# Scores and values times W1 in eight array tiles of 64 rows by 32 columns, and the token work over two tiles at once

## The chip, the cores and the metric

The kernel runs on one core of a Trainium2 chip. The metric is the device time in microseconds (us). Before the change three runs gave 532.68 us (median; 532.6 to 533.12). TensorE is PE in the profile (PEld is its loading of weights), VectorE is DVE, ScalarE is ACT, GpSimd is POOL, SyncE is SP; SP issues nearly all loads, POOL the stores of the output.

## The reference, cut to what matters

Attention over 32 memory slots per head, then a mixture of experts with one expert per token:

```
a   = softmax of phi over the 576 positions           # 8 batches, 8 heads, 576 x 32
k_m = a.T @ k ; v_m = a.T @ v                         # 32 x 64 per head
s   = softmax over the 32 slots of (q @ k_m.T / 8)    # 576 x 32 per head
x   = s @ v_m, the heads side by side                 # 4608 tokens x 512
logits = cosine of x with 8 expert vectors / tau ; e = argmax ; gate = softmax at e
out = gate * (relu(x @ w1[e]) @ w2[e])                # w1 512 x 1024, w2 1024 x 512
```

## The kernel before

One batch of 576 tokens goes through three stages.

`memories(b)` (lines 203 to 274) turns the exponentials of phi (`te`), multiplies them with k and v in column tiles of 32 (`slots`, line 219, tile `acc`), scales (`block`, lines 229 and 230) and turns the result per head pair (`flip`), so that `kT` and `vT` hold for each head pair c a 128-row block: rows 0 to 63 the first head's 64 features, rows 64 to 127 the second's, with columns for 32 slots of each and zeros in the two off-diagonal quarters.

`tokens(b)` (lines 276 to 401) works on five tiles of 128 tokens (`T0`; the fifth overlaps the fourth by half). `scores(i)` multiplies q (as weights, 128 x 128) with `kT` (64 columns) for four head pairs, line 291; DVE takes the maximum and subtracts it, ACT the exponential (lines 295 to 298). `weights(i)` divides by the sum (303 to 306). `turn(i)` transposes the weights on PE (312); ACT copies them to `ah` and DVE takes the rest `al` (315, 316), two parts so that a product in the faster 32-bit form keeps its accuracy. `attend(i)` (325) multiplies them with `vh`, `vl`, and DVE forms the logits and norms (328 to 331). Then follow the choice of the expert (`key`, 352 to 365) and the gates (374 to 400).

The expert's stage is where the values enter: `first` (432 to 466) computes G = `vT` times W1 (line 441, tile `pg`, four PSUM tiles of 512 columns, two column tiles of 64 each), splits it into `gh` (ACT, 444) and `gl` (DVE, 445), and multiplies G with the weights of the tokens (line 454, tile `ph`, 16 groups of six matmuls). ACT and DVE form relu and its rest (457, 458). `second` (468 to 482) multiplies with W2 (line 476, tile `py`, five tiles of 8 x 3 matmuls), ACT scales by the gate (480), POOL stores (488). W2 is split by `split_w` within `first`.

Order: everything is written out by hand. The loop of lines 613 to 631 runs `first(b)` and `second(b)` and, after each group of matmuls in `first` and each second one in `second` (each one in batch 0), takes one step of the generator `ahead(b)`, which runs `memories(b+2)` and `tokens(b+2)`; a step is what lies between two `yield`s. The four `pg` groups of batches 1 and later have no such steps between them. All engines work through their instructions in the order written. Every matmul on plain 32-bit numbers counts as two instructions of PE.

PSUM holds two buffers for the attention (`pt`), three for `pg`, `ph` and `py` (`mm`), two banks `po` for `attend` and one for `acc`.

Of the kernel before, what the change touches and what calls it, by code (L numbers as in the profile page):

```python
# [30 lines left out]
def sqrt(nc, pool, out, ss, shape, tag):  # L31
# [6 lines left out]
    for k in range(3):  # L38
        nc.vector.reciprocal(out=r, in_=a)
        nc.vector.scalar_tensor_tensor(out=r, in0=r, scalar=0.5, in1=ss, op0=ALU.mult, op1=ALU.mult)  # L40
        nc.vector.scalar_tensor_tensor(out=out if k == 2 else a, in0=a, scalar=0.5, in1=r, op0=ALU.mult, op1=ALU.add)


class Kernel:
# [4 lines left out]
    def __init__(self, ctx, tc, phiT, qT, kv, kvt, emb, tau, w1, w2, out):  # L49
# [20 lines left out]
        self.kT = st([P, NC, D], F32, name="kT")  # L70

# [45 lines left out]
    def load_router(self):  # L117
        nc, st = self.nc, self.st.tile
        self.em = st([E, DM], F32, name="em")
        nc.scalar.dma_start(self.em, self.emb)  # L120
        self.tv = st([E, 1], F32, name="tv")
        nc.scalar.dma_start(self.tv, self.tau.broadcast_to((E, 1)))

    def router(self):
# [4 lines left out]
        sq = st([E, DM], F32, name="sq")  # L129
# [34 lines left out]
    def load_q(self, b):  # L164
        if b < B:
            self.nc.sync.dma_start(self.q(b), self.qT[b])
# [36 lines left out]
    def memories(self, b, pt):  # L203
# [11 lines left out]
        def slots(g, *ks):  # L215
            for k in ks:
# [40 lines left out]
        slots(1, 2, 3, 4)  # L257
        block(1)
        self.load_kv(b + 1)
        yield  # L260
# [15 lines left out]
    def tokens(self, b):  # L276
# [3 lines left out]
        qt = self.q(b)  # L280
        a = {}
        lg = wk([P, NT, E], F32, tag="lg", name=f"lg{b}")
        ss = wk([P, NT], F32, tag="ss", name=f"ss{b}")

# [15 lines left out]
        def weights(i):  # L300
            x = a[i]
            z = wk([P, H], F32, tag="z", name=f"z{b}_{i}")
# [5 lines left out]
        def turn(i):  # L308
            t = self.pt([P, NG, P], f"ta{b}_{i}")
            x = a[i]  # L310
            for g in range(NG):
                nc.tensor.transpose(t[:, g], x[:, 4 * g : 4 * g + 4].rearrange("p h m -> p (h m)"), self.ident)
            o = P if i < 4 else 64
            to = slice(T0[i] + P - o, T0[i] + P)
            nc.scalar.copy(ah[:, :, to], t[:, :, P - o :])
            nc.vector.tensor_tensor(out=al[:, :, to], in0=t[:, :, P - o :], in1=ah[:, :, to].bitcast(F32), op=ALU.subtract)

        def attend(i):

            po = self.po[:, i % 2, : NC * (D + E)]  # L320
            to = slice(T0[i], T0[i] + P)
            for g in range(NG):
                w = slice(2 * g * (D + E), 2 * (g + 1) * (D + E))
                for k, (x, v) in enumerate(((ah, self.vh), (al, self.vh), (ah, self.vl))):
                    nc.tensor.matmul(po[:, w], lhsT=x[:, g, to], rhs=v[:, w], start=k == 0, stop=k == 2)  # L325
            po = po.rearrange("p (c m) -> p c m", c=NC)
            x = a.pop(i).rearrange("p (c j) m -> p c (j m)", c=NC)
            nc.vector.tensor_reduce(out=lg[:, i], in_=po[:, :, D:].rearrange("p c e -> p e c"), axis=AX.X, op=ALU.add)
            nc.vector.tensor_reduce(out=m[:, i : i + 1], in_=lg[:, i], axis=AX.X, op=ALU.max)
            nc.vector.tensor_scalar(out=oh[:, i], in0=lg[:, i], scalar1=m[:, i : i + 1], scalar2=None, op0=ALU.is_equal)  # L330
            nc.vector.tensor_tensor_reduce(  # L331
                out=x, in0=po[:, :, :D], in1=x, scale=1.0, scalar=0.0, op0=ALU.mult, op1=ALU.add, accum_out=ss[:, i : i + 1]
            )

        m = wk([P, NT], F32, tag="m", name=f"m{b}")
        oh = wk([P, NT, E], BF16, tag="oh", name=f"oh{b}")

        key = self.po[:, 1, 504:]
        for k in range(NT + 4):
            if k < NT:  # L340
                scores(k)
            if 0 <= k - 1 < NT:
                weights(k - 1)
            if k < NT + 3:
                yield
            if 0 <= k - 2 < NT:
                turn(k - 2)
            if 0 <= k - 3 < NT:
                attend(k - 3)
            if k == NT + 3:  # L350
                for i in range(-1, NT):
# [312 lines left out]
```

## Time and profile before

| | us |
|---|---|
| median of three runs | 532.68 |
| the profiled execution | 532.79 |
| its span | 530.8 |
| busy PE, DVE, ACT within the span | 495.4, 309.7, 199.8 |

The span is from the first to the last instruction of the program that the profile shows; 1.99 us of the profiled execution lie around it. The busy time of PE counts a matmul from its start to its modelled end, so that consecutive matmuls overlap: what a matmul costs is read from the distance between the starts.

### The profile page before, as it was taken

The numbers are of one execution on the slowest core, as the hardware profiler recorded it, in microseconds if no ns is written. First come the engines' busy times: TensorE is split into PE (matmuls) and PEld (weight loads), VectorE is DVE, ScalarE is ACT, GpSimd is POOL, SyncE is SP. The second block draws the span as 40 slices with busy tenths as digits, with TensorE's granted clock in tenths as the row PEclk, the third lists the DMA queues.
The fourth block names the chain that finished last, engine by engine and source line by source line (L and its number), as shares of the span: only waits on it lengthen the run. The fifth ranks groups of instructions, "written<-read, shape, count | busy, mean of one in ns | idle before, by whom it ended". The sixth has DMA issues, their size and how long they took to land.

```text
span 530.8 us, 9294 instructions
## 1 busy us (share of the span) xinstructions
PE 495.4 (93%) x3396; PEld 406.1 (76%) x3396; DVE 309.7 (58%) x1016; ACT 199.8 (38%) x509; POOL 23.7 (4%) x48
## 2 busy tenths in 40 slices
PE   4685987998999999999999999999999999999994
PEld 3574676786788877988788877988788878887883
DVE  4677868187368636775468636776468548206500
ACT  4332435222563226522563226522563127216411
POOL 1000000000000010000000010000000010010000
PEclk9877877999999999999999999999999999999998
DMA  8976345960595319571595319571525117610011
GB/s 270 343 259 225 107 153 198 328 223 38 187 297 186 132 41 329 182 248 41 178 307 186 130 41 326 184 249 41 184 88 176 42 40 249 199 59 12 10 51 32
DMA packets 36817, 87.18 MB, mean 164 GB/s; under 512 B 7832, under 2 KB 7832, under 8 KB 35744
## 3 DMA queue, kind: packets, MB, share of 16 engines
q1 hardware_dynamic: 33792, 77.08, 43.6%
q0 software_dynamic: 2944, 9.44, 5.0%
q8 instruction: 29, 0.48, 0.4%
q14 instruction: 20, 0.16, 0.1%
q10 hardware_dynamic: 32, 0.02, 0.0%
HBM read 66.60 MB, written 19.92 MB: 163 GB/s over the span
## 4 chain that ended last, share of the span: by engine, by line
issue 62%; PE 20%; DVE 10%; POOL 3%; ACT 2%; DMA 1%; SPq 0%; POOLq 0%; ACTq 0%; DVEq 0%
PE py L476 7%; PE ph L454 4%; POOL out_dram L488 3%; PE sc L291 2%; PE acc L219 2%; PE po L325 2%; PE pg L441 1%; DMA kl<-kvt 1%; DVE ea L306 1%; PE te L212 1%; DVE ea L297 1%; DVE z L303 1%; DVE ea L331 1%; DVE hl L458 1%; DVE mx L295 1%
## 5 line engine op out<-in xcount | busy, mean ns | idle before, releaser
L476 PE MATMUL py<-wh,hh 128*128 128x512 f32 x320 | 130.7, 408 | 0.0
L476 PE MATMUL py<-wh,hl 128*128 128x512 f32 x320 | 125.3, 392 | 0.0
L476 PE MATMUL py<-wl,hh 128*128 128x512 f32 x320 | 125.2, 391 | 0.0
L454 PE MATMUL ph<-aT,gh 128*128 128x288 f32 x512 | 113.8, 314 | 4.1 <-DVE hl L458 4.1
L454 PEld LDWEIGHTS ph<-aT,gh 128*128 128x128 f32 x512 | 82.5, 193 | 15.2 <-DVE gl L445 5.7
L458 DVE SCALAR_TENSOR_TENSOR hl<-ph,hh 128x288 fp32r<-128x288 f32 x128 | 57.6, 454 | 34.1 <-ACT hh L457 31.4
L454 PE MATMUL ph<-aT,gl 128*128 128x288 f32 x256 | 76.6, 299 | 0.0
L480 ACT ACTIVATE ys<-py,gate 128x512 f32<-128x512 f32 x40 | 27.4, 685 | 126.1 <-PE py L476 70.1
L476 PEld LDWEIGHTS py<-wh,hl 128*128 128x128 f32 x320 | 60.4, 189 | 13.3
L476 PEld LDWEIGHTS py<-wh,hh 128*128 128x128 f32 x320 | 60.5, 189 | 10.9 <-issue 1.0
L476 PEld LDWEIGHTS py<-wl,hh 128*128 128x128 f32 x320 | 60.6, 190 | 9.8
L457 ACT ACTIVATE hh<-ph 128x288 fp32r<-128x288 f32 x128 | 52.1, 412 | 28.1 <-PE ph L454 28.0
L445 DVE TENSOR_TENSOR gl<-pg,gh 128x512 fp32r<-128x512 f32 x32 | 22.1, 691 | 65.9 <-ACT gh L444 65.9
L454 PEld LDWEIGHTS ph<-aT,gl 128*128 128x128 f32 x256 | 49.3, 193 | 0.0
L430 DVE TENSOR_TENSOR wl<-w2s,wh 128x512 fp32r<-128x512 f32 x64 | 44.2, 690 | 2.5
L488 POOL DMA_DIRECT2D out_dram<-ys x40 | 22.0, 550 | 500.8 <-ACT ys L480 428.8
L298 ACT ACTIVATE ea<-ea 128x256 f32<-128x256 f32 x40 | 16.7, 417 | 62.8 <-DVE ea L297 62.8
L291 PEld LDWEIGHTS sc<-kT,qt 128*128 128x128 f32 x280 | 36.2, 196 | 4.2 <-issue 1.8
L429 ACT CAST wh<-w2s 128x512 fp32r<-128x512 f32 x64 | 39.3, 614 | 0.0
L291 PE MATMUL sc<-kT,qt 128*128 128x64 f32 x280 | 36.5, 275 | 0.8 <-DVE vl L273 0.4
L325 PE MATMUL po<-vh,aT 128*128 128x144 f32 x160 | 31.6, 292 | 4.5 <-DVE ss L331 4.0
L441 PE MATMUL pg<-w1s,vT 128*64 128x512 f32 x128 | 31.7, 630 | 0.0
(112 smaller groups left out, 520.1 us busy)
## 6 DMA issues: line engine op xcount, KB each, us to landing
kx<-kv SPq DMA_DIRECT2D x64, 256.0 KB, 5.3
w1s<-w SPq DMA_DIRECT2D x32, 512.0 KB, 5.7
w2s<-w SPq DMA_DIRECT2D x32, 512.0 KB, 4.9
ad<-aT SPq DMA_DIRECT2D x16, 576.0 KB, 6.7
out_dram<-ys POOLq DMA_DIRECT2D x32, 256.0 KB, 2.3
qt<-qT SPq DMA_DIRECT2D x7, 1152.0 KB, 5.6
ex<-phiT SPq DMA_DIRECT2D x16, 288.0 KB, 3.6
kl<-kvt SPq DMA_DIRECT2D x16, 128.0 KB, 5.0
```

Of the source, the lines that this page charges most:

```text
L291: nc.tensor.matmul(sc[:, 2 * c : 2 * c + 2], lhsT=qt[:, c, T0[i] : T0[i] + P], rhs=self.kT[:, c], start=True, stop=True)
L325: nc.tensor.matmul(po[:, w], lhsT=x[:, g, to], rhs=v[:, w], start=k == 0, stop=k == 2)
L429: self.nc.scalar.copy(self.wh[:, j], self.w2s[:, j])
L430: self.nc.vector.tensor_tensor(out=self.wl[:, j], in0=self.w2s[:, j], in1=self.wh[:, j].bitcast(F32), op=ALU.subtract)
L441: nc.tensor.matmul(p[64 * k : 64 * k + 64], lhsT=vT[:, 2 * g + k, :D], rhs=self.w1s[:, 2 * g + k, f], start=True, stop=True)
L445: nc.vector.tensor_tensor(out=gl[:, g, f], in0=p, in1=gh[:, g, f].bitcast(F32), op=ALU.subtract)
L454: nc.tensor.matmul(p, lhsT=w[:, g, fs], rhs=x[:, g, to], start=g == 0 and k == 0, stop=g == 1 and k == 2)
L457: nc.scalar.activation(self.hh[:, f, to], p, AF.Relu)
L458: nc.vector.scalar_tensor_tensor(out=self.hl[:, f, to], in0=p, scalar=0.0, in1=self.hh[:, f, to].bitcast(F32), op0=ALU.max, op1=ALU.subtract)
L476: nc.tensor.matmul(p, lhsT=h[:, f, to], rhs=w[:, f], start=f == 0 and k == 0, stop=f == 7 and k == 2)
L480: nc.scalar.activation(y, p, AF.Copy, scale=gate[:, i : i + 1])
L488: self.nc.gpsimd.dma_start(self.out[r + o : r + P], y[o:])
```

## The change

Scores: q becomes the moving operand. For each head one matmul with 64 rows (its features) and 32 columns (its slots) runs over 512 tokens, then a second piece over the last 64; the result, slots by tokens, is copied by ACT to `sT` and transposed on PE into tokens by slots (`weigh`). The eight heads lie on eight different tiles of the array. To that end heads 4 to 7 have their two halves of the 128 rows exchanged: in `block` for k and v, and in the loads of q, W1 and the expert vectors, which become three DMAs for two (or for one).

Values times W1: the same eight tiles, in a function `project` of its own; it runs for batch b+1 within `second(b)` (after steps 19 and 27 of 40, in place of a step of `ahead` there in batch 0), for batch 0 ahead of the loop. W1 is loaded at the start of `first(b)`; W2 of batch 0 is loaded and `keep(0)` done right after the scores of batch 1.

Token work: tiles 0 and 1, 2 and 3, and 4 alone go through `weigh`, `divide`, `turn` and `attend` together; one DVE or ACT instruction covers both tiles of a pair (except the last of `attend`, one per tile), and `po` is used in both banks by a pair. `tokens` has 18 steps in place of 22, `memories` 13 in place of 12; in `memories` the products of a head group stand in one step.

```diff
+PAIRS = ((0, 1), (2, 3), (4,))
...
+def halves():
+
+    lo, hi = slice(0, 64), slice(64, 128)
+    return (slice(0, P), slice(0, P), slice(0, 2)), (lo, hi, slice(2, 4)), (hi, lo, slice(2, 4))
...
     def load_q(self, b):
         if b < B:
-            self.nc.sync.dma_start(self.q(b), self.qT[b])
+            for dst, src, c in halves():
+                self.nc.sync.dma_start(self.q(b)[dst, c], self.qT[b, src, c])
...
     def load_w1(self, e):
-        nc = self.nc
         for h in range(2):
-            for g in range(NG):
-                c, f = slice(2 * g, 2 * g + 2), slice(h * 512, h * 512 + 512)
-                nc.sync.dma_start(self.w1s[:, c, f], self.w1[bass.ds(e, 1), :, c, f].rearrange("a p c f -> (a p) c f"))
+            f = slice(h * 512, h * 512 + 512)
+            for dst, src, c in halves():
+                self.nc.sync.dma_start(
+                    self.w1s[dst, c, f], self.w1[bass.ds(e, 1), src, c, f].rearrange("a p c f -> (a p) c f")
+                )
...
-            nc.vector.tensor_scalar(out=kb[:, g], in0=self.acc[:, :, :D], scalar1=r, scalar2=None, op0=ALU.mult)
-            nc.scalar.activation(vb[:, g], self.acc[:, :, D:], AF.Copy, scale=r)
+            k, v = (x[:, g].rearrange("p (k i) d -> p k i d", i=2)[:, :, :: 1 - 2 * g] for x in (kb, vb))
+            a = self.acc.rearrange("p (k i) d -> p k i d", i=2)
+            nc.vector.tensor_scalar(out=k, in0=a[..., :D], scalar1=r, scalar2=None, op0=ALU.mult)
+            nc.scalar.activation(v, a[..., D:], AF.Copy, scale=r)
...
-        slots(0, 0, 1)
-        yield
-        slots(0, 2, 3, 4)
+        slots(0)
         block(0)
         yield
-        slots(1, 0, 1)
+        yield
         yield
         flip(0)
         yield
-        slots(1, 2, 3, 4)
+        slots(1)
         block(1)
         self.load_kv(b + 1)
+        yield
         yield
         yield
         flip(1)
...
-        def scores(i):
-            sc = self.pt([P, H, M], f"sc{b}_{i}")
-            for c in range(NC):
+        def scores(t0, t1):
+
+            ts = [self.pt([P, t1 - t0], f"ts{b}_{t0}{g}") for g in range(NG)]
+            for h in range(H):
+                g, j = divmod(h, 4)
+                c, i = divmod(h, 2)
+                r = slice(64 * (i ^ g), 64 * (i ^ g) + 64)
                 nc.tensor.matmul(
-                    sc[:, 2 * c : 2 * c + 2], lhsT=qt[:, c, T0[i] : T0[i] + P], rhs=self.kT[:, c], start=True, stop=True
+                    ts[g][32 * j : 32 * j + 32],
+                    lhsT=self.kT[r, c, 32 * i : 32 * i + 32],
+                    rhs=qt[r, c, t0:t1],
+                    start=True,
+                    stop=True,
                 )
-            mx = wk([P, H], F32, tag="mx", name=f"mx{b}_{i}")
+            for g in range(NG):
+                nc.scalar.copy(sT[:, g, t0:t1], ts[g])
+
+        def weigh(p):
+            ti = PAIRS[p]
+            n = len(ti)
+            sc = self.pt([P, n, H, M], f"sc{b}_{p}")
+            for k, i in enumerate(ti):
+                for g in range(NG):
+                    nc.tensor.transpose(
+                        sc[:, k, 4 * g : 4 * g + 4].rearrange("p h m -> p (h m)"), sT[:, g, T0[i] : T0[i] + P], self.ident
+                    )
+            sc = sc.rearrange("p k h m -> p (k h) m")
+            mx = wk([P, 2 * H], F32, tag="mx", name=f"mx{b}_{p}")[:, : n * H]
             nc.vector.tensor_reduce(out=mx, in_=sc, axis=AX.X, op=ALU.max)
-            a[i] = x = wk([P, H, M], F32, tag="ea", name=f"ea{b}_{i}", bufs=5)
+            a[p] = x = wk([P, 2 * H, M], F32, tag="ea", name=f"ea{b}_{p}", bufs=3)[:, : n * H]
...
+        def attend(p):
+
+            ti = PAIRS[p]
+            n, i = len(ti), slice(ti[0], ti[-1] + 1)
+            po = self.po[:, :n, : NC * (D + E)]
+            for k in range(n):
+                to = slice(T0[ti[k]], T0[ti[k]] + P)
+                for g in range(NG):
+                    w = slice(2 * g * (D + E), 2 * (g + 1) * (D + E))
+                    for l, (x, v) in enumerate(((ah, self.vh), (al, self.vh), (ah, self.vl))):
+                        nc.tensor.matmul(po[:, k, w], lhsT=x[:, g, to], rhs=v[:, w], start=l == 0, stop=l == 2)
+            po = po.rearrange("p t (c m) -> p t c m", c=NC)
+            x = a.pop(p).rearrange("p (t c j) m -> p t c (j m)", t=n, c=NC)
+            nc.vector.tensor_reduce(
+                out=lg[:, i], in_=po[..., D:].rearrange("p t c e -> p t e c"), axis=AX.X, op=ALU.add
...
+        scores(0, 512)
+        yield
+        scores(512, S)
+        if b == 0:
+            self.load_q(2)
+        elif b >= 2:
+            self.load_q(b + 1)
+        yield
+        for k in range(len(PAIRS) + 3):
+            if k < len(PAIRS):
+                weigh(k)
+            if 0 <= k - 1 < len(PAIRS):
+                divide(k - 1)
+            if k < len(PAIRS) + 2:
                 yield
+            if 0 <= k - 2 < len(PAIRS):
                 turn(k - 2)
+            if 0 <= k - 3 < len(PAIRS):
                 attend(k - 3)
+            if k == len(PAIRS) and b >= 1:
                 self.softmax(b + 1)
             yield
...
-    def first(self, n, at, vT):
+    def project(self, n, vT):
+
+        nc = self.nc
+        for k in range(2):
+            f = slice(512 * k, 512 * k + 512)
+            ps = [self.mm([P, 512], f"pg{n}_{k}{g}") for g in range(NG)]
+            for h in range(H):
+                g, j = divmod(h, 4)
+                c, i = divmod(h, 2)
+                r = slice(64 * (i ^ g), 64 * (i ^ g) + 64)
+                nc.tensor.matmul(
+                    ps[g][32 * j : 32 * j + 32],
+                    lhsT=vT[r, c, 32 * i : 32 * i + 32],
+                    rhs=self.w1s[r, c, f],
+                    start=True,
+                    stop=True,
+                )
+            for g in range(NG):
+                nc.scalar.copy(self.gh[:, g, f], ps[g])
+                nc.vector.tensor_tensor(
+                    out=self.gl[:, g, f], in0=ps[g], in1=self.gh[:, g, f].bitcast(F32), op=ALU.subtract
+                )
+            yield
+
+    def first(self, n, at):
 
         nc = self.nc
...
-        if n >= 5:
+        if n == 0 or n >= 4:
             steps(mem)
     for _ in mem:
         pass
     tok = k.tokens(1)
-    steps(tok, 5)
+    steps(tok, 2)
+    k.load_w2(k.expert(0))
+    k.keep(0)
+    steps(tok, 3)
+    for _ in k.project(0, k.vT[0]):
+        steps(tok)
     left = None
     for b in range(B):
         att = k.ahead(b, tok)
         tok = None
-        for n, _ in enumerate(k.first(b, k.aT[b % 2], k.vT[b % 2])):
-            if n == NG * 2 - 1 and 1 <= b < B - 1:
-                k.load_w1(k.expert(b + 1))
-            if n >= NG * 2 or b == 0:
-                steps(att)
-            if b == 0 and n == NG * 2:
-                k.load_w2(k.expert(0))
-                k.keep(0)
+        if 1 <= b < B - 1:
+            k.load_w1(k.expert(b + 1))
+        for _ in k.first(b, k.aT[b % 2]):
+            steps(att)
         if b + 1 < B:
             k.load_w2(k.expert(b + 1))
             k.keep(b + 1)
+        pro = k.project(b + 1, k.vT[(b + 1) % 2]) if b + 1 < B else iter(())
         for n, _ in enumerate(k.second(b, k.gate[:, b], k.rows(b))):
-            if b == 0 or n % 2 == 0:
+            if n in (19, 27):
+                steps(pro)
+            elif b == 0 or n % 2 == 0:
                 steps(att)
         for _ in att:
             pass
```

The functions `divide` and `turn` are the former `weights` and `turn` over a pair; `softmax(b+1)` stays behind the first `attend`. `em` and the square of the expert vectors now lie in `sT`.

## Rows read from the trace of the kernel before

**Rows 1.** The profile's page: busy time by engine, and granted clock in 40 slices.
```profile
PE 495.4 (93%) x3396; PEld 406.1 (76%) x3396; DVE 309.7 (58%) x1016; ACT 199.8 (38%) x509; POOL 23.7 (4%) x48
...
PEclk9877877999999999999999999999999999999998
```

**Rows 2.** Batches 1 and 6: length; busy PE, PEld, DVE, ACT, POOL; clock; DMA, GB/s.
```profile
137.32:197.05 59.73, 59.61 (x425) 49.22 (x424) 38.31 (x124) 24.53 (x63) 2.73 (x5) 1.00 0.54 183
...
436.02:479.75 43.73, 43.73 (x234) 36.23 (x233) 14.98 (x28) 15.73 (x33) 2.73 (x5) 1.00 0.46 154
```

**Rows 3.** Timeline of PE into batch 4: start, us, instruction, count.
```profile
316.03 0.39 PE L476 MATMUL py<-wl,hh 128*128 128x512 f32 x1
316.26 0.39 PE L476 MATMUL py<-wh,hl 128*128 128x512 f32 x1
316.58 3.65 PE L441 MATMUL pg<-w1s,vT 128*64 128x512 f32 x16
320.16 0.53 PE L454 MATMUL ph<-aT,gh 128*128 128x288 f32 x2
```

**Rows 4.** Timeline of PE, windows 316.70 to 317.00 and 324.66 to 324.70.
```profile
316.58 0.65 PE L441 MATMUL pg<-w1s,vT 128*64 128x512 f32 x2
...
324.61 0.32 PE L219 MATMUL acc<-kx,eT 128*32 128x128 f32 x4
```

**Rows 5.** Timeline of PE in batch 4: products of `memories`, transposes, scores.
```profile
321.06 0.60 PE L212 MATMUL te<-ident,ex 128*128 128x128 f32 x4
321.41 0.51 PE L454 MATMUL ph<-aT,gh 128*128 128x288 f32 x2
...
324.61 0.64 PE L219 MATMUL acc<-kx,eT 128*32 128x128 f32 x16
325.19 0.53 PE L454 MATMUL ph<-aT,gh 128*128 128x288 f32 x2
...
341.58 0.39 PE L476 MATMUL py<-wh,hl 128*128 128x512 f32 x1
341.81 1.00 PE L291 MATMUL sc<-kT,qt 128*128 128x64 f32 x8
342.62 0.48 PE L476 MATMUL py<-wh,hh 128*128 128x512 f32 x1
342.93 0.39 PE L476 MATMUL py<-wl,hh 128*128 128x512 f32 x1
```

**Rows 6.** Groups by line and shape: count, busy us, mean ns, then idle before.
```profile
L480 ACT ACTIVATE ys<-py,gate 128x512 f32<-128x512 f32 x40 | 27.4, 685 | 126.1 <-PE py L476 70.1 <-issue 51.3 <-PEq L506 4.8
...
L445 DVE TENSOR_TENSOR gl<-pg,gh 128x512 fp32r<-128x512 f32 x32 | 22.1, 691 | 65.9 <-ACT gh L444 65.9
...
L295 DVE TENSOR_REDUCE mx<-sc 128x8 f32<-128x256 f32 x40 | 16.7, 417 | 7.9 <-PE sc L291 7.7
...
L213 ACT COPY eT<-te 128x512 f32<-128x512 f32 x16 | 9.4, 588 | 1.5 <-PE te L212 1.4
```

**Rows 7.** Waits of PE in window 16 to 137: us, times, longest.
```profile
PE sc L291 <- DVE ea L297: 5.7, 2, 5.4
PE ph L454 <- DVE hl L458: 4.1, 3, 2.2
PE po L325 <- DVE ss L331: 4.0, 5, 1.5
```

**Rows 8.** Timeline of PE in batch 0.
```profile
51.65 1.98 PE L441 MATMUL pg<-w1s,vT 128*64 128x512 f32 x4
53.55 0.69 PE L312 MATMUL ta<-ident,ea 128*128 128x128 f32 x2
...
61.19 0.51 PE L454 MATMUL ph<-aT,gh 128*128 128x288 f32 x2
...
90.45 0.78 PE L476 MATMUL py<-wh,hh 128*128 128x512 f32 x1
```

More of the change, by code (lines that the diff above doesn't have):

```diff
@@ L118, in load_router @@
         nc, st = self.nc, self.st.tile
-        self.em = st([E, DM], F32, name="em")
-        nc.scalar.dma_start(self.em, self.emb)
+        self.em = self.sT[:E, 0, :DM]
+        src, dst = (x.rearrange("e (c i d) -> e c i d", c=NC, i=2) for x in (self.emb, self.em))
+        nc.scalar.dma_start(dst[:, :2], src[:, :2])
+        for i in range(2):
+            nc.scalar.dma_start(dst[:, 2:, i], src[:, 2:, 1 - i])
         self.tv = st([E, 1], F32, name="tv")
@@ L213, in turn, with slots @@
             nc.scalar.copy(eT[:, i0:i1], t[:, : i1 - i0])
-        def slots(g, *ks):
-            for k in ks:
+        def slots(g):
+            for k in range(5):
                 src = self.kx[k] if k < 4 else self.kl
@@ L279, in tokens @@
         ah, al = self.aT[b % 2]
-        qt = self.q(b)
+        qt, sT = self.q(b), self.sT
         a = {}
@@ L306, in weights @@
             nc.vector.tensor_tensor(out=x, in0=x, in1=b3(z, M), op=ALU.mult)
[L308 to L332, printed above, removed]
-            )
@@ L335, in tokens, with turn @@
[L335 to L344, printed above, removed]
+        def turn(p):
+            ti = PAIRS[p]
+            t = self.pt([P, NG, len(ti) * P], f"ta{b}_{p}")
+            for k in range(len(ti)):
+                for g in range(NG):
+                    x = a[p][:, H * k + 4 * g : H * k + 4 * g + 4].rearrange("p h m -> p (h m)")
+                    nc.tensor.transpose(t[:, g, k * P : k * P + P], x, self.ident)
+            o = 0 if p < 2 else 64
+            to = slice(T0[ti[0]] + o, T0[ti[-1]] + P)
+            nc.scalar.copy(ah[:, :, to], t[:, :, o:])
+            nc.vector.tensor_tensor(out=al[:, :, to], in0=t[:, :, o:], in1=ah[:, :, to].bitcast(F32), op=ALU.subtract)
@@ new lines, in attend @@
+        def attend(p):
+            ti = PAIRS[p]
+            n, i = len(ti), slice(ti[0], ti[-1] + 1)
[10 more added lines that the diff above has]
+                out=lg[:, i], in_=po[..., D:].rearrange("p t c e -> p t e c"), axis=AX.X, op=ALU.add
+            )
+            nc.vector.tensor_reduce(out=m[:, i], in_=lg[:, i], axis=AX.X, op=ALU.max)
+            nc.vector.tensor_tensor(out=oh[:, i], in0=lg[:, i], in1=b3(m[:, i]), op=ALU.is_equal)
+            for k in range(n):
+                nc.vector.tensor_tensor_reduce(
+                    out=x[:, k],
+                    in0=po[:, k, :, :D],
+                    in1=x[:, k],
+                    scale=1.0,
+                    scalar=0.0,
+                    op0=ALU.mult,
+                    op1=ALU.add,
+                    accum_out=ss[:, ti[k] : ti[k] + 1],
+                )
@@ L349, in tokens @@
                 attend(k - 3)
-            if k == NT + 3:
-                for i in range(-1, NT):
-                    nc.tensor.matmul(
-                        key, lhsT=self.ones, rhs=self.eb if i < 0 else oh[:, i], start=i < 0, stop=i == NT - 1
-                    )
-            if k == NT - 1:
-                if b == 0:
-                    self.load_q(2)
-                elif b >= 2:
-                    self.load_q(b + 1)
-            if k == NT and b >= 1:
+            if k == len(PAIRS) and b >= 1:
@@ L361, in tokens @@
                 self.softmax(b + 1)
             yield
+        for i in range(-1, NT):
+            nc.tensor.matmul(key, lhsT=self.ones, rhs=self.eb if i < 0 else oh[:, i], start=i < 0, stop=i == NT - 1)
         ki = wk([1, 1], I32, tag="ki", name=f"ki{b}")
@@ L430, in split_w @@
         self.nc.vector.tensor_tensor(out=self.wl[:, j], in0=self.w2s[:, j], in1=self.wh[:, j].bitcast(F32), op=ALU.subtract)
[L432 removed]
+    def project(self, n, vT):
[14 more added lines that the diff above has]
+                )
+            for g in range(NG):
+                nc.scalar.copy(self.gh[:, g, f], ps[g])
+                nc.vector.tensor_tensor(
+                    out=self.gl[:, g, f], in0=ps[g], in1=self.gh[:, g, f].bitcast(F32), op=ALU.subtract
+                )
+            yield
+    def first(self, n, at):
         nc = self.nc
         gh, gl, (ah, al) = self.gh, self.gl, at
[L436 to L446 removed]
         for s in range(2):
@@ L575, in rest @@
                 nc.vector.scalar_tensor_tensor(out=ix, in0=tok, scalar=bc, in1=ex, op0=ALU.add, op1=ALU.add)
-                for _ in self.first("r", at, vT):
+                for _ in self.project("r", vT):
+                    pass
+                for _ in self.first("r", at):
                     pass
```

25 lines of the change are left out of this document (8 added, 17 removed).

## Prediction

> **What bounds the kernel now.** I read the page first, then windows cut where a batch's first `pg` starts, then the timeline of PE in one batch, its waits, and the groups by shape for durations. The page shows PE busy for 93% of the span and at nine tenths of the full clock (2.4 GHz) or more from the eighth slice on, 93 us; ahead of that the granted clock is lower, down to 0.7 in a slice [rows 1]. The windows say that batches 1 to 5 take 59.7 us each at a granted clock of 1.00 (five rows from 59.71 to 59.77; one stands) with PE busy in all but 0.1 us of it, while DVE is busy for 38 us and ACT for 25; batch 6, which has no attention beside it, takes 43.7 us, all PE [rows 2]. So from 137 us on only fewer or shorter PE instructions make it faster, and anything that makes PE wait makes it slower by as much. The stretch before, up to 137 us, is a mixture: the PE waits of any length lie there, for DVE in nearly all cases [rows 7].
>
> **W1 in `project`.** The 16 `pg` instructions start at 316.58; with the last `py` at 316.26 and 0.23 us between `py` starts (316.03, 316.26), the engine is free at 316.49, and the next stage starts at 320.16: 3.67 us a batch [rows 3]. In the window 316.70 to 317.00 exactly two instructions are under way [rows 4], the two column tiles of 64; 16 instructions in 3.58 us are so 8 rounds of 0.45 us. After the change there are 16 instructions per half of the 1024 columns, on eight tiles: if all eight run beside each other, two rounds, 0.9 us, and I add 0.25 for entering and leaving (0.09 before the first `pg`, and 0.08 that the first matmul behind another kind costs: 342.62 to 342.93 is 0.31 against 0.23 [rows 5]) and for eight starts. Two halves: 2.3 us, a gain of 1.4 us for each of 8 batches. That four tiles run beside each other is seen: four `acc` instructions are under way together [rows 4]. That two tiles in different row halves do is seen nowhere before; the bounds are two rounds (0.9 us) and four (1.8 us), and I take two, since the tiles that the trace shows never delay each other. The drain by ACT and DVE (0.59 and 0.69 us each for 512 columns [rows 6]) moves from the start of `first` into `second`, where both have room.
>
> **Scores.** Now a tile costs 342.62 less 341.81 (0.81), plus 0.08: 0.89 us, five times 4.45 us a batch [rows 5]. After: one piece of 512 tokens as above, 1.15 us; one of 64 tokens, 16 instructions again: at least two rounds of an eighth (0.11 us), at most 0.75 us, what the 16 `acc` instructions of 128 columns take with their edges (325.19 less 324.61, and 0.17) [rows 5]; I take 0.45, the middle. And ten transposes: four `te` take 321.41 less 321.06, 0.35 us, with the edge 0.43 [rows 5]; two fours and a two are 1.1 us. Sum 2.7 us, a gain of 1.75 us a batch.
>
> **Fewer changes of kind.** `slots` of a head group stands in one step instead of two, and `turn` and `attend` in 4 places instead of 6. Each place saved is 0.17 us of edges; 0.5 us a batch with the shorter `attend` sequences counted as nothing.
>
> **Token work on DVE and ACT.** An instruction of 256 elements takes 0.42 us (`mx`), one of 512 takes 0.69 [rows 6]: two become one for 0.15 us less, seven times for two pairs, so about 2 us less of DVE a batch; ACT gets four copies (two of 0.59 and two short ones, some 1.6 us) and joins two pairs of instructions twice. In batches 1 to 5 that gains nothing by itself, since neither bounds.
>
> **New waits.** (a) The second piece of the scores needs the two PSUM buffers that the first piece filled, so PE waits for two copies of 0.59 us on ACT [rows 6] and 0.2 until the first can begin, with one `ph` group of 0.9 us in between (six matmuls, 320.16 to 321.06 [rows 3, 5]): 0.5 us. (b) A pair takes both banks of `po`. `attend(2)` can start only when DVE has read the pair before, and DVE stands behind `softmax(b+1)`, which waits for ACT. I take 0.9 us, near the mean of the five waits of `po` for `ss` in the stretch before 137 us (4.0 over 5 [rows 7]). Behind the waiting matmul stand the `py` matmuls, so PE stands still. Together 1.4 us a batch. Bounds: nothing, for PE has no such wait in batches 1 to 5 today [rows 2]; and 1.5 us at each of five places, as the longest wait of `po` for `ss` in batch 0 [rows 7], 7.5 us. I take the low one, because in batches 1 to 5 the steps lie two `py` triples (1.4 us) apart, and in batch 0 one.
>
> So a batch of 1 to 5 gains 1.4 + 1.75 + 0.5 - 1.4 = 2.2 us, five times 11 us; batch 6 gains 1.4.
>
> **Up to 137 us.** In batch 0 W1 ran at half clock: four instructions from 51.65 to 53.55, and four such parts with token work between them, until the first `ph` at 61.19 [rows 8]. After: two parts of 2.1 us at that clock in place of four of 1.9, and shorter DVE work on the tiles around them; that is 7.6 against 4.2, a gain of 3.4. The token work that stands with them has some ten DVE instructions fewer, 1.5 us. So I put the first `ph` 5 us earlier, at 56. From there to the first `py` at 90.45 [rows 8] PE waits for DVE [rows 7], which has the same splits, gates and relu rests to do: nothing. `second(0)` then holds W1 of batch 1 in its shorter form (1.4) and shorter scores, but with a step after each `py` triple the pairs wait longer: a gain of 2 with W1. Together 7 us, between none (if the chain of DVE sets the time as before) and 12 (if all of batch 0's token work shrinks as its instruction count). W1, q and the expert vectors take 3 DMAs for 2 or 1; W1 is issued a whole `first` ahead of its use, so that costs nothing in batches 1 to 5; for batch 0 it is two issues more on SP, under 1 us, inside these bounds.
>
> **Sum.** 11 + 1.4 + 7 = 19.4 us off the profiled execution, 532.79 us (0.11 over the median of the three runs): 513.4, say 513 us.
>
> **Rivals.**
> *Row halves one after the other.* Heads 0 to 3 write one PSUM bank from both row halves. If tiles of different halves wait for each other there, each piece takes four rounds: 0.9 us more, twice per batch for W1 and once, with 0.1 for the short piece, for the scores: 2.8 a batch, 14 us over five, 1.8 in batch 6, 4 before: 533 us, no change. For it: no row here shows two row halves at once. Against: the four column tiles show no coupling. The Trainium skill, TensorEngine Tiling (Array Packing), section Restrictions and Gotchas, says under PSUM pressure that different row tiles write different banks and can't access the same bank at the same time; by that rule this rival would be the outcome, and no row here tests it, as all tiles before have 128 rows.
>
> *The ring of three PSUM buffers.* `project` takes two of the three buffers while `py` fills the third. If buffers are handed out strictly in turn, the next `py` gets the one just filled and waits for ACT's `ys`, 0.69 us [rows 6], and some 0.2 of latency: 0.9 us twice in seven batches, 12.6 us: 526 us. For it: there are only three. Against: at that moment two are free or soon will be, if the next free one is taken.
>
> *Nothing waits.* The two waits cost nothing (7 us) and the start gains 12 in place of 7: 501 us. For it: PE has hardly a wait after 137 us now.
>
> *Slower: the pair chain stands in PE's order.* Weigh, divide, turn and attend of a pair are each twice as long on DVE and ACT, and PE meets them in the same order with the same few triples between. If each of five places waits 1.5 us, as `po` did once in batch 0 [rows 7], that is 7.5 in place of the 1.4 counted, 30 us over five batches: 544 us. It turns the sign from 3.9 us a batch beyond those counted (19.4 over five). Against: DVE has 21 us free in a batch.
>
> **How the numbers follow.** Forecast 0.50 (505 to 521 of its own), nothing waits 0.16, ring 0.12, row halves 0.13, pair chain 0.09. About 0.2% is what a measurement can tell from no change. Faster: 0.50 + 0.16 + 0.12 and 0.04 of the row halves, 0.82; same another 0.04 of them; slower 0.09 and their other 0.05, 0.14. The range, 500 to 532, holds the forecast, nothing waits and the ring, and reaches to the row halves.
>
> **What would show it.** `project` in two bursts of 1.1 to 1.2 us each, with eight matmuls under way at once (four: row halves in turn); `first` starting with `ph` right behind `py`; windows of batches 1 to 5 of 57.5 us; PE waits at the second piece of the scores (for ACT `sT`) and at `po` (for `ss`) of under 1 us each; no wait of `py` for `ys`; the first `ph` at about 56 us. It would be wrong if a burst takes 2 us, if PE waits add to over 4 us a batch, or if the granted clock falls below full after 100 us.

## The result and the profile after

The changed kernel takes 512.27 us (median; 511.03 to 514.8), the kernel before, measured beside it, 532.9: ratio 0.9613, 95% interval 0.9568 to 0.9658. The forecast was 513.0. The spans differ by 19.4 us (530.8 to 511.4), which is the forecast sum to the tenth; what follows shows that several of its terms were not. One of the six executions of `pg_wide` below took 933.54 us, for no reason that the record shows, and its ratio is taken without it.

The page after: TensorE is busy for 24 us less in sum; its granted clock is 8 or more tenths but for one slice, and from the eleventh slice (128 us) on 9 tenths or more up to the last slice (before: from the eighth, 93 us [rows 1]).

```profile
PE 471.0 (92%) x3540; PEld 378.3 (74%) x3540; DVE 285.9 (56%) x856; ACT 204.1 (40%) x509; POOL 23.7 (5%) x48
PEclk9988887998999999999999999999999999999998
```

Windows cut at a batch's first `ph`, for batches 1, 4, 6 and 7 (columns as in rows 2):

```profile
136.61:193.68 57.07, 56.70 (x444) 45.80 (x443) 35.38 (x104) 25.15 (x63) 2.73 (x5) 1.00 0.59 191
307.76:364.78 57.02, 56.65 (x443) 45.79 (x442) 35.38 (x104) 25.23 (x63) 2.73 (x5) 1.00 0.60 191
421.54:464.00 42.46, 42.46 (x249) 35.45 (x248) 14.80 (x28) 15.53 (x33) 2.73 (x5) 1.00 0.34 110
464.00:511.40 47.40, 40.10 (x217) 35.07 (x215) 12.22 (x24) 14.07 (x30) 3.29 (x6) 0.96 0.09 29
```

Against 59.73 and 43.73 [rows 2], batches 1 to 4 gain 2.7 us each and batch 5 3.0 (five together 13.8, from the first `ph` of batch 1 to that of batch 6); batch 6 gains 1.3. DVE has 2.9 us less to do in a batch. The remaining 4.3 us lie ahead of batch 1's first `ph` (140.91 to 136.61).

The timeline of PE around a burst of `project`, and the windows inside it with the count of `pg` under way:

```profile
291.12 0.40 PE L539 MATMUL py<-wh,hl 128*128 128x512 f32 x1
291.44 1.09 PE L492 MATMUL pg<-w1s,vT 64*32 64x512 f32 x16
292.46 0.50 PE L539 MATMUL py<-wh,hh 128*128 128x512 f32 x1
```

```profile
291.75:291.85 0.10, 0.10 (x8) 0.00 (x0) 0.00 (x0) 0.00 (x0) 1.00 0.00 0
291.95:292.00 0.05, 0.05 (x16) 0.00 (x0) 0.00 (x0) 0.00 (x0) 1.00 0.00 0
```

Eight instructions run at once, and the next eight begin before they end. The sixteen take 1.02 us up to the next `py`, which is two rounds. No `py` waits for a buffer.

The scores in batch 4, PE with the readers of `kk`, which stood one step ahead in the same pair of PSUM buffers (duration behind the start; idle time in brackets):

```profile
324.40 1.94 PE L313 MATMUL ts<-qt,kT 64*32 64x512 f32 x16
324.56 0.27 ACT L286 CAST vh<-kk 64x144 fp32r<-64x144 f32 x1 [0.75 <-DVE vl L287]
324.86 0.31 DVE L287 TENSOR_TENSOR vl<-kk,vh 64x144 fp32r<-64x144 f32 x1 [0.34 <-ACT vh L286]
325.25 0.18 PEld L313 LDWEIGHTS ts<-qt,kT 64*32 64x32 f32 x8 [0.69 <-issue]
326.27 0.54 PE L517 MATMUL ph<-aT,gh 128*128 128x288 f32 x2
327.27 0.34 PE L313 MATMUL ts<-qt,kT 64*32 64x64 f32 x16
327.54 0.53 PE L517 MATMUL ph<-aT,gh 128*128 128x288 f32 x2
```

The first piece takes 1.87 us up to the next `ph`, where the same sixteen instructions of `project` take 1.02. Its first eight instructions are heads 0 to 3, from both row halves, into the first of the two buffers; the second eight are heads 4 to 7, into the other, which `kk` held (the expectations below call these the second row half). The second eight weight loads start at 325.25, 0.08 us after the last `vl` is done (324.86 + 0.31). The list of waits does not have this one, since the first eight matmuls are still counted as busy. All that it has from 137 us on is:

```profile
PE po L369 <- DVE ss L378: 1.5, 4, 0.4
```

And in the window 16 to 137 us, beside [rows 7]:

```profile
PE po L369 <- DVE ss L378: 5.9, 5, 2.5
PE ts L313 <- ACT sT L321: 4.9, 2, 4.1
PE ta L353 <- DVE ea L345: 4.8, 4, 2.1
```

In batch 0 the granted clock falls once after 100 us, where the kernel before kept it (1.00 from 100 to 137 us in its profile, 0.95 here). The wait of PE just ahead of it, and the windows of the fall:

```profile
120.04 0.42 PE L369 MATMUL po<-vh,aT 128*128 128x144 f32 x2 [1.64 <-DVE ss L378]
```

```profile
120.00:124.00 4.00, 3.68 (x20) 2.96 (x21) 2.37 (x15) 0.48 (x1) 0.00 (x0) 0.80 0.00 0
124.00:128.00 4.00, 4.00 (x27) 2.48 (x26) 3.01 (x19) 0.44 (x2) 0.54 (x1) 0.78 0.83 259
```

Means of 0.80 and 0.78 between the two levels, 2.4 and 1.2 GHz, are some 3.4 us at the lower one, so by this estimate about 1.7 us of work is lost. The fall stands behind a pair's wait for `po`; that the wait is its cause was not tried. The profiles of `kk_two` and `joined` below show it too (0.95 from 100 to 137 us), that of `pg_wide`, which has the same pairs, does not (1.00).

The theory after this profile: the eight tiles and the scores give what was counted, the first score piece loses 0.85 us a batch to `kk`'s readers, and the 4.3 us at the start are set by a mixture of ACT, DVE and loads.

### The profile page after: what moved, and what is told of

Read it like the earlier page. It is cut to its first block, busy times and chain, and to the rows that moved or that the text cites. A ratio compares the mean times of both kernels' runs of the same rounds, so it can differ in the third digit from the quotient of the medians.

```text
span 511.4 us, 9479 instructions
## 1 busy us (share of the span) xinstructions
PE 471.0 (92%) x3540; PEld 378.3 (74%) x3540; DVE 285.9 (56%) x856; ACT 204.1 (40%) x509; POOL 23.7 (5%) x48
## 4 chain that ended last, share of the span: by engine, by line
issue 63%; PE 18%; DVE 10%; POOL 4%; ACT 2%; DMA 2%; SPq 0%; POOLq 0%; ACTq 0%; DVEq 0%
PE py L539 6%; PE ph L517 4%; POOL out_dram L551 4%; PE acc L232 2%; PE ts L313 1%; DVE ea L378 1%; ACT ex L210 1%; DMA w1s<-w 1%; DVE ea L336 1%; PE po L369 1%; PE sc L329 1%; DVE aT L357 1%; DVE ea L345 1%; DVE z L342 1%; DVE mx L334 1%
## 5 line engine op out<-in xcount | busy, mean ns | idle before, releaser
L517 PE MATMUL ph<-aT,gh 128*128 128x288 f32 x512 | 111.8, 311 | 2.6 <-DVE hl L521 2.6
L539 PEld LDWEIGHTS py<-wh,hl 128*128 128x128 f32 x320 | 60.5, 189 | 13.5
L480 DVE TENSOR_TENSOR wl<-w2s,wh 128x512 fp32r<-128x512 f32 x64 | 44.2, 691 | 3.0
L501 DVE TENSOR_TENSOR gl<-pg,gh 128x512 fp32r<-128x512 f32 x32 | 20.6, 685 | 31.1 <-ACT gh L500 31.0
L369 PE MATMUL po<-vh,aT 128*128 128x144 f32 x160 | 29.1, 281 | 7.6 <-DVE ss L378 7.4
L369 PEld LDWEIGHTS po<-vh,aT 128*128 128x128 f32 x160 | 24.3, 191 | 11.0 <-issue 9.6
L500 ACT CAST gh<-pg 128x512 fp32r<-128x512 f32 x32 | 17.1, 588 | 35.3 <-PE pg L492 35.3
L337 ACT ACTIVATE ea<-ea 128x512 f32<-128x512 f32 (+1 forms) x24 | 13.5, 561 | 38.4 <-DVE ea L336 38.4
L369 PE MATMUL po<-vl,aT 128*128 128x144 f32 x80 | 22.1, 276 | 0.0
```

What stands on the lines that cost most here:

```text
L337: nc.scalar.activation(x, x, AF.Exp, scale=1.0 / 8.0)
L369: nc.tensor.matmul(po[:, k, w], lhsT=x[:, g, to], rhs=v[:, w], start=l == 0, stop=l == 2)
L480: self.nc.vector.tensor_tensor(out=self.wl[:, j], in0=self.w2s[:, j], in1=self.wh[:, j].bitcast(F32), op=ALU.subtract)
L500: nc.scalar.copy(self.gh[:, g, f], ps[g])
L501: nc.vector.tensor_tensor(out=self.gl[:, g, f], in0=ps[g], in1=self.gh[:, g, f].bitcast(F32), op=ALU.subtract)
L517: nc.tensor.matmul(p, lhsT=w[:, g, fs], rhs=x[:, g, to], start=g == 0 and k == 0, stop=g == 1 and k == 2)
```

## Experiments

Every run is compared with the kernel before, measured beside it; windows and starts come from the one profiled execution of each.

**W1 in the old form, new place (`pg_wide`).**

```
-for h in range(H): ps[g][32*j:32*j+32] = vT[r, c, 32*i:32*i+32] x w1s[r, c, f]
+for c in range(NC): ps[g][64*i:64*i+64] = vT[:, c, :D] x w1s[:, c, f]
```

> `project` stands where the change put it, but each instruction takes all 128 rows and 64 columns, as before the change (8 instructions a burst in program order, 16 on the engine). Theory A (the eight tiles give the gain): four rounds of 0.45 us in place of two, so each burst grows from 1.0-1.1 to about 1.9 us; two bursts a batch give back 1.5 to 1.8 us, seven batches at full clock some 11 us and batch 0 at its lower clock 2: 523 to 526 us against 512.3 for the changed kernel, windows of 58.6 us in place of 57.0. Rival B (the gain of W1 comes from its new place, the bursts were never four rounds long): under 515 us.

522.25 us, ratio 0.9803 (0.9761 to 0.9846). A burst and a batch's window:

```profile
293.91 1.94 PE L490 MATMUL pg<-w1s,vT 128*64 128x512 f32 x8
295.78 0.50 PE L533 MATMUL py<-wh,hh 128*128 128x512 f32 x1
```

```profile
311.95:370.74 58.79, 58.42 (x428) 46.39 (x427) 35.59 (x104) 25.45 (x63) 2.75 (x5) 1.00 0.58 185
```

A: 1.87 us a burst for 1.02, twice, and 1.75 us a batch. The form of the product is worth that much in this place. The total lies a little under A's range of 523 to 526: from the first `ph` of batch 0 to that of batch 1 this profile has a granted clock of 0.96, where the change's has 0.91, and takes 76.3 us for 79.8.

**W1 in the new form, old place (`pg_first`).**

```
+if b: run project(b) whole, ahead of load_w1(b + 1) and first(b)
-second(b): steps 19 and 27 run project(b + 1)
```

> The eight-tile `project` of batches 1 to 7 goes back to the start of `first`, with the load of the next W1 behind it. Theory A (the place is part of the gain): `first` now meets the drain. The second burst needs a PSUM buffer that ACT and DVE free 1.3 us after the first burst (0.59 + 0.69), and the first `ph` needs the `gl` of both groups; PE stands still for about 1.5 us a batch, 7 batches: 521 to 525 us, with PE waits at `pg` or `ph` for `gl`. Rival B (the place costs nothing, as the prediction took it): 511 to 514 us.

522.05 us, ratio 0.9785 (0.974 to 0.983). Window of batch 4, and the `project` ahead of it with its wait:

```profile
315.66:373.89 58.23, 57.33 (x447) 46.00 (x443) 35.50 (x105) 25.15 (x63) 2.73 (x5) 1.00 0.58 187
```

```profile
311.85 0.39 PE L539 MATMUL py<-wh,hl 128*128 128x512 f32 x1
312.17 1.96 PE L492 MATMUL pg<-w1s,vT 64*32 64x512 f32 x24
314.66 1.06 PE L492 MATMUL pg<-w1s,vT 64*32 64x512 f32 x8 [0.53 <-DVE gl L501]
```

A in kind, 1.2 us a batch in size for the 1.5 expected. Seven of these are 8 us; another 3.7 come from batch 0, whose first `ph` is at 60.49 us here although its `project` was not touched (two waits for DMA of 2.0 and 2.3 us; more on this below). Four rounds a burst had covered the drain by ACT and DVE; two do not. From the last `py` (311.85, and 0.23) to the first `ph` (315.66) this W1 takes 3.6 us, where the old form took 3.67 [rows 3]. So left where it was, the short form would have gained next to nothing; the whole change would have kept the other 1.5 of its 2.7 us.

**Scores in the old form (`sc_direct2`).**

```
-scores(0, 512), scores(512, S) into sT; weigh transposes sT
+weigh: sc[:, k, 2*c:2*c+2] = qt[:, c, T0[i]:T0[i]+P] x kT[:, c]; load_q(b + 1) behind the last
```

> Scores as before the change: q as weights, 128 rows by 64 columns of keys, token tile by token tile straight into the tile `sc`; no `sT`, no copies; the pairs stay, and the next batch's q is loaded behind the last tile's scores, as before the change. Theory A (the scores gain as predicted, 1.75 us a batch): batches 2 to 5 at 58.7 us, 512.3 + 7 to 10 = 519 to 522 us. Theory B (the first score piece stands 1.9 us where 1.1 was predicted, so that the new scores cost 3.4 us a batch against 4.3): 57.9 us a batch for the four batches beside which a later one's scores run, and batch 1 ahead of 57 us saves its 4 us wait for the copies `sT`: 512 to 516 us.

529.51 us; the total can't be read. q of batch 1 lies in `w2s`, its scores now come behind the load of W2 that overwrites it, so that they are computed from W2's data, and PE waits 15.3 us for that load. (A first form, 589.15 us, took a later batch's q in most batches and is not read at all.) The windows of later batches hold:

```profile
PE sc L316 <- DMA w2s<-w: 15.4, 2, 15.3
```

```profile
324.09:381.99 57.90, 57.52 (x442) 48.69 (x440) 35.32 (x104) 23.84 (x59) 2.73 (x5) 1.00 0.61 188
```

57.90, as B said: the scores as they stand in the change give 0.85 us a batch, half of the forecast term. (The run keeps the pairs, so that its old scores stand in three places, where the kernel before had five.) What they are worth ahead of 137 us stays open.

**One token tile at a time (`singles`).**

```
-PAIRS = ((0, 1), (2, 3), (4,))
+PAIRS = ((0,), (1,), (2,), (3,), (4,));  po = self.po[:, p % 2 : p % 2 + 1, ...]
```

> The token work runs over one tile at a time again, as before the change (two banks of `po` in turn), with the new scores and the new `project`. Theory A (pairs save edges on PE and time on DVE that only counts ahead of 137 us): windows of batches 1 to 5 longer by 0.5 us at most, the first `ph` of batch 0 at 59 to 60 us in place of 56.8: 515 to 519 us. Rival B (the pairs are a burden on PE, by the double wait at `po`): under 511.5 us.

519.21 us, ratio 0.9761 (0.9722 to 0.98), just above A's range. Batches 1 to 4 take 57.4 us, the first `ph` of batch 0 is at 57.97 and that of batch 1 4.4 us later than in the change. From 141 us on, PE waits longer with single tiles than with pairs; the window is that of batch 4:

```profile
PE po L369 <- DVE ss L378: 2.7, 4, 0.7
313.19:370.54 57.35, 56.67 (x443) 45.60 (x442) 38.11 (x124) 25.65 (x67) 2.73 (x5) 1.00 0.59 191
```

The pairs are worth 0.3 us in each of batches 1 to 4, and all of it is this wait: PE is busy for 56.67 us here and for 56.65 in the change, so that they save it no edges that show. In batch 5, where single tiles have no wait left, they are the shorter form (56.46 for 56.76). In batch 0 they are worth up to 4 us, where DVE is busy for 6.1 us longer without them from the first `ph` of batch 0 to that of batch 1; but 1.6 us of `pg` waiting for W1, which the change's profile does not have, stand ahead of it. As for the rival of the pair chain, the pairs shorten the wait that it feared.

**`kk` further ahead of the scores (`kk_early`, `kk_two`).**

```
 flip(1)
 yield
-yield
 kk ...
 yield
+yield      # kk_early
+yield      # kk_two has this one as well
```

> In `memories`, `kk` is issued one step earlier (one `ph` group, 0.9 us) and a step is left empty behind it; nothing else moves. Theory A (the second row half of the first score piece waits for the PSUM buffer that `kk` holds until its fourth reader is done, 325.17 against the piece's start at 324.40): the piece takes 1.1 us in place of 1.94, windows of batches 1 to 5 shorter by 0.8 us: 508 to 509.5 us. Rival B (the piece is slow by itself, its row halves stand in each other's way): 1.9 us still, 511.5 to 513 us.

> `kk` one step earlier, as in the run `kk_early`, and the scores and all behind them one step later: two `ph` groups more between `kk` and the first score piece. Theory A (the piece waits for the last reader of `kk`, which in `kk_early` was done 0.4 us after the piece began): the piece falls from 1.57 to 1.1 us, windows of batches 1 to 5 from 56.67 to 56.2-56.3 us, the time 2 us under `kk_early`. Rival B (the second row half of a piece starts later by itself): still 1.5 to 1.6 us and 56.7 us a batch.

`kk_early`: 511.3 us, ratio 0.9588 (0.9565 to 0.9612); `kk_two`: 508.23, ratio 0.9519 (0.949 to 0.9547). The first score piece of batch 4 and the windows, first of `kk_early`, then of `kk_two`:

```profile
320.97 1.57 PE L313 MATMUL ts<-qt,kT 64*32 64x512 f32 x16
321.06 0.31 DVE L286 TENSOR_TENSOR vl<-kk,vh 64x144 fp32r<-64x144 f32 x1 [0.34 <-ACT vh L285]
321.44 0.18 PEld L313 LDWEIGHTS ts<-qt,kT 64*32 64x32 f32 x8 [0.32 <-issue]
...
304.33:361.00 56.67, 56.30 (x443) 45.78 (x442) 35.39 (x104) 25.04 (x63) 2.73 (x5) 1.00 0.60 192
```

```profile
323.14 1.09 PE L314 MATMUL ts<-qt,kT 64*32 64x512 f32 x16
324.26 1.07 ACT L322 COPY sT<-ts 128x512 f32<-128x512 f32 x2 [0.30 <-PE ts L314]
325.15 0.55 PE L314 MATMUL ts<-qt,kT 64*32 64x64 f32 x16
325.64 0.50 PE L540 MATMUL py<-wh,hh 128*128 128x512 f32 x1
...
305.71:361.60 55.89, 55.89 (x444) 45.77 (x442) 35.30 (x104) 25.11 (x63) 2.75 (x5) 1.00 0.61 195
```

One step was not enough: the last `vl` is done at 321.37, 0.4 us after the piece began, and again the second loads start 0.07 behind it; the total of `kk_early` can't be told from the changed kernel's. With two steps the piece takes 1.09 us; nothing of it is slow by itself. That is 0.85 of the 1.2 us a batch. The `po` waits, 0.37 us in each of batches 1 to 4, are gone too: the list has no wait of PE from 137 us on, and PE counts as busy for the whole window. But 0.2 us is lost again, in the same unlisted way: the second piece takes 0.49 us up to the next `py` where it took 0.27 in the change, and the second copy `sT`, which empties the buffer that its second eight need, ends at 325.33 (324.26 + 1.07), within the piece. Rival B is out, and my size for `kk_early` (0.8) was wrong, because `kk`'s four readers, which go in turns on ACT and DVE, were done 2.6 us behind the start of `kk` there (318.76) against 2.2 in the change (323.00), so that 0.8 us of lead became 0.4.

**Batch 0: four edits ahead of 57 us.**

`exp_first`, in which `sq` goes behind `softmax(0)`:

> The square of the expert vectors (`sq`, ACT) is issued behind the two exponentials of batch 0's softmax in place of ahead of them. Theory A (the table load and `sq` wait for the last of the three loads of `emb`, until 4.68, and the exponentials stand behind them): first `te` at 5.5 us in place of 7.6, and all that follows up to 57 us is a chain, so 510 us. Rival B (the first `te` comes at 5.5, but `acc` waits for the keys and values, or the chain of DVE is the same length): 512 us.

513.37 us, ratio 0.9627 (0.9605 to 0.9649): no gain. The first `te` comes 1.5 us earlier (2.1 expected), the first `ph` of batch 0 no earlier (57.56); PE waits for loads instead:

```profile
PE te L225 <- ACT ex L210: 6.1, 1, 6.1
PE pg L492 <- DMA w1s<-w: 2.4, 1, 2.4
PE ts L313 <- DMA qt<-qT: 1.1, 1, 1.1
```

`gate0`, in which the token steps of batch 0 behind `fl` are issued ahead of `second(0)`:

> The last steps of batch 0's token work (the root of `ss` and the gate, some 20 DVE instructions at 42 to 47 us) are issued ahead of `second(0)`, whose output is the first to need them. Theory A (the 4.1 us wait of PE at 48.41 for the copies `sT` comes from them: `vl` stands behind them on DVE, and `sT` behind `vh` on ACT): that wait falls under 1 us and the first `ph` of batch 0 comes 3 to 4 us earlier, at 53 to 54; the end 1 to 3.5 us earlier: 509 to 511 us. Rival B (the load of W1 for batch 0 sets when `project(0)` starts): the first `ph` stays at 56 to 57 and the time at 512.

516.28 us, ratio 0.9682 (0.9656 to 0.9708): slower, which neither theory had. A's wait did go (4.1 to 0.8 us), and the scores of batch 1 were done 2.7 us earlier, but `project(0)` then met W1 on its way, three times:

```profile
45.69 0.93 PE L313 MATMUL ts<-w2s,kT 64*32 64x64 f32 x16 [0.76 <-ACT sT L321]
51.41 1.06 PE L492 MATMUL pg<-w1s,vT 64*32 64x512 f32 x8 [1.04 <-DMA w1s<-w]
53.62 1.57 PE L492 MATMUL pg<-w1s,vT 64*32 64x512 f32 x8 [1.14 <-DMA w1s<-w]
56.49 1.93 PE L492 MATMUL pg<-w1s,vT 64*32 64x512 f32 x8 [1.31 <-DMA w1s<-w]
58.70 0.83 PE L517 MATMUL ph<-aT,gh 128*128 128x288 f32 x2
```

From the first `ph` of batch 0 to that of batch 1 it takes another 2 us longer (81.8 for 79.8). This profile also has the lower granted clock, 0.81 for 0.88 in the change up to the first `ph` and 0.88 for 0.91 behind it, so that what W1, the gate's instructions in their new place and the clock cost is not separated.

`one_dma`, in which q and W1 lie in memory with the halves already changed over (one load for three), and `late_kv`, in which `load_kv(2)` and `load_q(2)` stand behind `keep(0)`:

> q and W1 are laid out in memory with the two halves of rows of chunks 2 and 3 already changed over, so that the loads are whole again: one DMA for q and four for W1, in place of three and six. Theory A (the DMAs of W1 for batch 0 set when `project(0)` starts, and two issues of 0.74 us less bring them earlier): the first `ph` of batch 0 at 55 to 56 us, no waits of `pg` or `ts` for a DMA, 510 to 511.5 us; batches 1 to 5 as they are, 57.05. Rival B (the engines of the DMAs are full and the bytes the same): 512 to 513 us.

> The keys, values and q of batch 2 (3.6 MB, ten DMAs and three) are issued behind W1, W2 and the stores of batch 0 in place of ahead of them; they are needed only from 90 us on. Theory A (up to 57 us the DMA engines are full, share 0.85 to 1.05, so that W1 and q(1) come late because of the bytes ahead of them): W1 lands 3 to 6 us earlier, waits of `pg` for `w1s` go, and the first `ph` comes 1 to 3 us earlier: 509 to 511 us. Rival B (the wait of `ts` for `sT` at 48 us, behind the gate of batch 0 on DVE, sets the time whatever the loads do): 511.5 to 513 us.

511.24 us, ratio 0.9582 (0.9549 to 0.9615), and 511.86, 0.9598 (0.9565 to 0.9631): neither can be told from the changed kernel, so the times decide between no theories. Their issue queues did move, from 43.75 for W1's first load in the change to

```profile
41.90 2.63 SPq L188 DMA_DIRECT2D w1s<-w  x4
```

```profile
40.70 4.37 SPq L188 DMA_DIRECT2D w1s<-w  x6
```

but only `one_dma` has W1 earlier: the last load of it is issued at 44.2 and takes 7.0 us to land, at 51.2. In `late_kv` that is 44.5 and 9.8, at 54.3, where the change has 47.6 and 6.9, at 54.5: with batch 2's keys, values and q no longer ahead of it, W1 lands no earlier in this profile, so A of `late_kv` is out on that point. The 4.1 us wait for `sT` stands in both, and the first `ph` comes at 55.36, as A of `one_dma` said, and 56.60.

**`joined`**: `kk_two`, `one_dma`, `late_kv` and `exp_first` together.

> Four edits together: `kk` one step earlier and the scores one later (`kk_two`), q and W1 laid out so that they load whole (`one_dma`), batch 2's keys, values and q behind batch 0's W1 and W2 (`late_kv`), and `sq` behind the exponentials (`exp_first`). Theory A (the loads ahead of 57 us hide what the earlier `te` gives): batches 1 to 5 at 55.85 us as in `kk_two`, 6 us off; first `ph` of batch 0 at 53 to 55 us, 2 to 4 off: 502 to 505 us. Rival B (the wait of `ts` for `sT` behind batch 0's gate sets the first 57 us whatever the loads do): first `ph` at 55.4 or later, 505.5 to 508 us.

504.1 us, ratio 0.9461 (0.9424 to 0.9497), in A's range: all six times (503.3 to 504.9) lie under all six of `kk_two` (506.5 to 509.5). The first `ph` is at 54.04, where `kk_two` has it at 58.8; no PE wait for a DMA is left in the list, and what stands is

```profile
PE po L369 <- DVE ss L378: 6.1, 5, 2.5
PE te L223 <- ACT ex L208: 6.1, 1, 6.1
PE ta L353 <- DVE ea L345: 4.0, 4, 1.3
PE ts L313 <- ACT sT L321: 3.7, 2, 3.0
```

So three edits of which none gave a measurable gain alone give 3 to 4 us beside `kk_two` (4.1 by the medians, 3.1 by the ratios). What fits is that up to 57 us each was hidden behind one of two others, the loads and the chain on ACT and DVE. But `kk_two` has 2.9 us of `pg` waiting for W1 in its profile (last load landed at 56.5; 50.2 in `joined`), so loading W1 in whole rows may do most of it. Which of the three is needed was not tried, nor `gate0` on top of them.

## Why the prediction was right, and where its terms were not

**W1 (1.4 us a batch): right, 0.2 short.** Two rounds a half, 1.02 us and 0.20 for entering and leaving (0.09 behind a `py` pitch of 0.23, and a first `py` that stands 0.11 longer): 2.44 a batch where 2.3 was forecast and 3.67 was before [rows 3], 1.2 us. The old product in the new place costs 1.75 more than the new one (`pg_wide`). That the drain costs nothing held, but only for the new place: left at `first` it costs 1.2 (`pg_first`), nearly all that the form gains.

**Scores (1.75): mis-sized; 0.85 in the change.** The second piece (0.27 and its edges, 0.45 forecast) and the transposes (four in 0.35 us, as `te` [rows 5]: the first pair's start at 328.44, the next `py` at 328.79) are as forecast. The first piece is 1.87 for 1.15, by `kk`'s readers. The forecast listed who waits for the buffers *behind* the first piece, the second piece, and did not ask who had them ahead. Without that wait the term would be 0.85 + 0.85 = 1.7; `kk_two`, which takes it away, pays 0.2 of it at the second piece.

**Changes of kind (0.5): not isolated.** `singles` undoes the pairs, and PE's busy time does not grow in batches 1 to 5; the step of `slots` was not tried by itself. What is left for this term, 0.9, comes out under "A batch".

**New waits (1.4 off).** (a) The wait of the second piece for the first (0.5) is not there in the change, neither in the list nor in the length of the piece (0.27); in `kk_two`, where the first piece is quick, it is 0.2. (b) `po` for `ss` is 0.3 a batch (1.5 us over the span) for 0.9. In their place stands 0.85 at the first piece. So 1.15 of 1.4: the size was near, the place was not, and that the error in the scores and that in the waits cancel is luck. Counting both, scores less waits: forecast 0.35, measured 0.85 less 0.3.

**A batch.** The forecast was 2.2, the windows show 2.7. W1 is 1.2 of it and the scores 0.85; idle time of PE takes 0.25 away (0.37 for 0.12 [rows 2]). That leaves 0.9 which no run isolates, for the changes of kind and the fewer places of the scores, where 0.5 was forecast: most of what the forecast fell short by lies in this term. (The losses in `pg_wide`, `sc_direct2` and `singles`, 1.75, 0.85 and 0.3, sum to 2.9 only because the old product costs more in the new place than in its old one, 3.67; the 0.3 is waiting.)

**Up to the first `ph` of batch 1 (7): 4.3.** The three parts: the first `ph` of batch 0 comes at 56.82 (56 forecast; 61.19 before [rows 8]), a gain of 4.4 for 5. From there to the first `py` "nothing" was forecast; it is 3.3 us longer (32.6 for 29.3), and in it PE runs 194 instructions in place of 145, and DVE is busy 2.0 us longer: steps of the token work and of `memories` that stood in `second(0)` before now fall into it. `second(0)` gains them back: 47.2 for 50.5, 3.2 us where 2 was forecast. The two DMAs more for W1, put at under 1 us, were the weakest number: the last load of it lands at 54.5 where it landed at 52.2 before. The changed kernel's profile shows no wait for it; those of `pg_wide`, `pg_first` and `exp_first` show 2.3 to 3.3 us of `pg` for `w1s`, and the first `ph` of batch 0 then comes at 57.6 to 60.5.

**The sum** was right to the tenth by luck: 13.8 for 11 in batches 1 to 5 met 4.3 for 7 at the start. The clock, which was to stay full after 100 us, did not (the 1.7 us above), and a fall was named as a sign of being wrong; its cost lies inside `second(0)`.

**Rivals.** *Row halves one after the other* is out: eight at once and 1.02 us, where four rounds take 1.87 (`pg_wide`). The Trainium skill, TensorEngine Tiling (Array Packing), section Restrictions and Gotchas, says that different row tiles can't access one PSUM bank at the same time; here heads 0 to 3 write one bank from both row halves, each 32 partitions of its own, and heads 4 to 7 another, and the trace shows all eight at once and no time spent on it: the measurement decides. The Trainium skill there leaves it to software to keep them apart and states no waiting, so that the prediction, which let this rival follow from it, read more into it than it says. *The ring* is out: no `py` waits for `ys`. *Nothing waits* is what `kk_two` comes near in batches 1 to 5, with 55.85 us. *The pair chain* is out by `singles`.

## What to carry to other kernels

When an instruction needs two buffers of a ring, look at who held them before it as well as at who gets them next; a wait in the middle of a group of matmuls appears in no list of waits, only as a group that is longer than its like. Here the shorter product uncovered the drain that its longer form hid, so form and place were one change. Where two chains of nearly the same length end at one point, an edit to one of them can measure as nothing until the other is shortened too; `joined` fits that, and does not prove it.

## What was not expected of the hardware

Eight tiles of 64 rows by 32 columns, writing two PSUM banks from both row halves, ran sixteen 512-column instructions in 1.02 us at a granted clock of 1.00. Their starts inside a round of eight lie so close that all eight are under way in the window of 0.1 us shown above.

When W1 for batch 0 lands differs between executions of kernels that load it alike: from issue to landing its last load takes 6.9 us in the changed kernel and 9.4 in `kk_two`, which issues it 0.4 us earlier (at 47.1), and PE waits for W1 not at all in the one and 2.9 us in the other. In the changed kernel the DMA engines are nearly full from 30 to 60 us; their busy tenths in 40 slices of that stretch:

```profile
DMA  9999999999999899994388998999999999999999
```

That the bytes of batch 2 make W1 late does not fit `late_kv`, which takes them out of the way and has the last load of W1 land at 54.3, as the change has (54.5). What goes with an early landing is the form of the load: 50.2 to 52.2 in `joined`, `one_dma` and the kernel before, which load it in four pieces of 128 rows, 54.3 to 58.2 in all runs with six pieces, four of them of 64 rows (the last issued at 44.5 to 50.2). It was not measured by itself.
